# An attention-then-Fourier-mix kernel on one core: second weights loaded in two pairs, and the opening batches' steps put in another order

## The chip, the core and the metric

The kernel runs on one core of a Trainium2 chip. The metric is device time in microseconds; the kernel before took 309.74 us, the median of 8 runs (307.34 to 312.01). A core has TensorE (PE, matrix multiplies into PSUM), VectorE (DVE), ScalarE (ACT), GpSimd (POOL) and SyncE (SP). Each engine takes its own instructions in the program's order and waits for the others by semaphores. Transfers between DRAM and the on-chip SBUF are issued by SP, ACT and POOL, and all run on the same 16 DMA engines.

## The reference

```python
# attention between x (8,8,512,64) and state (8,8,32,64), per batch and head
a     = softmax(x @ state.T / 8);   xread = a @ state
a2    = softmax(state @ x.T / 8);   sread = a2 @ x
x2    = concat(xread, sread)            # -> (8, 544, 512), heads side by side
# Fourier mix and a two-layer network
u     = x2 + real(fft(fft(x2, axis=1), axis=2))
un    = (u - mean) / sqrt(var + 1e-6)   # over the last axis
out   = u + relu(un @ w_ch1) @ w_ch2    # w_ch1 512 x 2048, w_ch2 2048 x 512
```

## The kernel before, in words

The work goes batch by batch, 0 to 7. For one batch b:

- **Load.** `load_x(b)` (L121) issues seven DMAs on SP into one of two `xs` buffers, in rows of 256 bytes. POOL casts it to bf16 into one of two `xin` buffers (`cast_x`, L148; for batch 2 `cast_columns`, L1117). For batches 2 and up, `turned[b]` (L560) issues DMA transposes on SP that give `sT` (state) and `xT` (x).
- **Attention** (`attend`, L360). The first stream holds `scores(0)`, `scores(1)` (matmuls L437, exponential on ACT L442), then `turn_scores(1)`, `turn_scores(0)` (matmuls with the identity L449, copied by ACT L450). `turn_scores` needs both exponentials. The second stream holds the reads: `read_low` (xread L462 into PSUM tile `xrp`, divided by DVE L470/L471 into `XR`, then POOL copies 32 rows of it into `XT`, L519), `fold_low` on POOL (L523 to L531), two reads into `XF`, `sread_by_head` (its L489 on DVE overwrites the rows of `XR` that `XT` was copied from, so it waits for POOL), and a last read followed by `fold()` (L536), twelve DVE operations that use the symmetry of the Fourier sums, from L534 to L549. In batches 0 and 1 a `state_rows` step on ACT (L515) overwrites those rows of `XR`, and the fold needs it.
- **Fourier mix** (`transform`, L698). `over_s(0..3)` (matmuls L783 on the fold's parts, ACT copies L784), `over_d(0..1)` (L679/L680 into `yp`), DVE adds x into `U` (L684, L691), statistics (L337/L339), centring into `ub` (ACT L840 for batch 1, DVE L842 later), and `turn_u`, the transposition into `unT` (TensorE L851 and a copy L852 for batches 0 and 1, SP DMA L847 later). Per batch there are four 128-row tiles (k, r).
- **Layer 1** (`layer1`, L914). 16 steps. Batch 0 uses `quarter_step` (L931): step L[4r+i] takes 16 matmuls of 128x128 (L936) of tile r, then ACT's ReLU L938. Other batches take 4 matmuls of 128x512 (L926) and L928. Each needs a PSUM tile `ph`.
- **Layer 2** (`layer2`, L947). For tile i four steps q of four 128x512 matmuls (L990) add up in one PSUM tile `po`; the last calls `store` (L952), whose DVE operation L957 scales, adds `U` and frees `po`. The output goes by SP, direct (L961) or through `r_dram` (L971, L972). For batch 0 the steps are called M[4i+q].

`ph` and `po` share the pool `psF`, which has three buffers; `xrp`, `xfp` and batch 2's scores share `psX`, which has one; the rest share `psQ`, which has three.

**What sets the order.** Every engine's order is the order in which the Python code emits the calls. Up to the first layer-2 steps it is written out by hand, L1024 to L1222. From there on each pass b of the loop at L1224 calls `weave` (L998): each stream is a list of steps with a start and an end between 0 and 1; the steps are spread evenly in that interval, and all are emitted in order of their place. Pass b runs layer 2 of batch b-1, layer 1 of b, reads and transform of b+1, scores of b+2, and the load of b+3. In pass 1 the remaining layer-2 steps are M[7] to M[15] (`l2_now`, nine).

**Weights.** POOL issues them as DMAs that cast float32 to bf16: `first_weights` (L310) four loads of w1, `second_weights` (L323, DMA L325) four of w2, each reading 1 MB and writing 512 KB. A `tensor_copy` into the tile `gate` on POOL holds POOL's queue back until the tile named in it is there: L1131 for the last w1 load, L1166 for batch 2's x, L1171 for the last w2 load. M with q = 0 needs the first w2 load, q = 1 the second, and so on.

**State.** `turn_in_dram(lo, hi)` (L154) copies state rows in reversed order from DRAM to DRAM (`s_dram`), `load_state` (L112) brings them in (tile `gen`), POOL casts them into `stb` (L168). For batch 2 this happens early (SP at 12.0 and 20.7 us); for batches 3 to 7 the copy goes out at 28.3, the load at 32.6, and POOL casts it after L1171. The eight `root` calls (L343/L344 on POOL) that L957 of batches 0 and 1 need follow that.

Of the kernel before, what the change touches and what calls it, by code (L numbers as in the profile page):

```python
# [30 lines left out]
def kernel(  # L31
# [8 lines left out]
    nc = tc.nc  # L40
# [71 lines left out]
    def load_state(lo, hi, src=state):  # L112
        nc.sync.dma_start(
            out=states(lo, hi).rearrange("p b g d -> p (b g) d"),
            in_=src[lo:hi].rearrange("b (g hh) j d -> (hh j) (b g) d", hh=4),
        )
# [4 lines left out]
    def load_x(b):  # L121
        xs = xs_of[b] if b in xs_of else wk.tile([128, 4 * dm], F32, name="xs", tag="xs")
        xs_of[b] = xs
        v = xs.rearrange("p (i h d) -> p i h d", i=4, d=D)
        xb = x[b].rearrange("h s d -> s h d")
        row = v[15:32:16, 3]
        parts = [
            (v[:, 0], xb[1:129]),
            (v[:, 1], xb[144:272]),
            (v[:, 2], xb[273:401]),  # L130
            (v[32:128, 3], xb[416:512]),
            (v[0:15, 3], xb[129:144]),
            (v[16:31, 3], xb[401:416]),
            (row, xb[0:273:272]),
        ]
        if b == 0:
            for queue, n in ((nc.sync, None), (nc.scalar, 2), (nc.sync, 3), (nc.scalar, 0), (nc.sync, 4), (nc.sync, 5), (nc.sync, 6),
                             (nc.sync, 1)):
                if n is None:
                    load_state(0, 1)  # L140
                else:
                    queue.dma_start(out=parts[n][0], in_=parts[n][1])
            return
        for o, rows in parts:
            nc.sync.dma_start(out=o, in_=rows)  # L145

    def cast_x(b, copy=nc.gpsimd.tensor_copy, lo=0, hi=4):
        copy(xin_bufs[b % 2][:, lo:hi, 1:513], xs_of[b].rearrange("p (i c) -> p i c", i=4)[:, lo:hi])  # L148
# [5 lines left out]
    def turn_in_dram(lo, hi):  # L154
        nc.sync.dma_start(out=s_dram[lo:hi].rearrange("b h j d -> (b h) j d"),
                          in_=state[lo:hi, :, ::-1, :].rearrange("b h j d -> (b h) j d"))
# [151 lines left out]
    def first_weights(lo, hi):  # L308
        for q in range(lo, hi):
            nc.gpsimd.dma_start(out=w1[:, :, q * 512:(q + 1) * 512], in_=w1v[:, :, q * 512:(q + 1) * 512])  # L310
# [9 lines left out]
    for lo, k0, c, t in ((0, 0, 3, 128.0), (128, 128, 3, 128.0), (256, 0, 4, 256.0), (384, 128, 5, pf[:, 6:7])):  # L320
        nc.gpsimd.tensor_scalar(gi[:, lo:lo + 128], in0=li[:, k0:k0 + 128], scalar1=pf[:, c:c + 1], scalar2=t,
                                op0=ALU.mult, op1=ALU.add)
    def second_weights():  # L323
        for q in range(4):
            nc.gpsimd.dma_start(out=w2[:, q * 4:(q + 1) * 4, :], in_=w2v[:, q * 4:(q + 1) * 4, :])  # L325
    def clear_state(lo, hi):
        nc.gpsimd.memset(stb[:, lo:hi].rearrange("p b g c -> p (b g c)").bitcast(F32), 0.0)
# [30 lines left out]
    turned = {}  # L358
# [588 lines left out]
    def layer2(key):  # L947
        steps = []
        n = 1 if isinstance(key, tuple) else 4
        po_of = {}  # L950

        def store(i, cols):  # L952
            u, rstd, dst = tiles_of[key][i]
            while later:
                later.pop()()
            ot = wk.tile([128, dm], F32, name="ot", tag="ot", bufs=4)
            nc.vector.scalar_tensor_tensor(ot[:, cols], in0=po_of[i][:, 0:cols.stop - cols.start], scalar=rstd,  # L957
                                           in1=u[:, cols], op0=ALU.mult, op1=ALU.add)
            queue = nc.scalar if key == B - 1 else nc.sync
            if isinstance(dst, bass.AP):  # L960
                nc.sync.dma_start(out=dst[:, cols], in_=ot[:, cols])  # L961
            elif isinstance(dst, int):
                nc.sync.dma_start(out=l_dram[dst].rearrange("b r n -> (b r) n"), in_=ot)
                for a in range(2):
                    nc.sync.dma_start(out=out[4 * dst:4 * dst + 4, 129 + 272 * a:144 + 272 * a, :].rearrange("b r n -> r b n"),
                                      in_=l_dram[dst, :, 16 * a:16 * a + 15, :].rearrange("b r n -> r b n"))
                    nc.sync.dma_start(out=out[4 * dst:4 * dst + 4, 272 * a, :].rearrange("b (c n) -> c b n", c=16),
                                      in_=l_dram[dst, :, 16 * a + 15, :].rearrange("b (c n) -> c b n", c=16))
            else:
                b, k, top = dst  # L970
                queue.dma_start(out=r_dram[b, k], in_=ot)  # L971
                later.append(lambda: queue.dma_start(  # L972
                    out=out[b, top:top - 128:-1, :].rearrange("r (c n) -> c r n", c=16),
                    in_=r_dram[b, k].rearrange("r (c n) -> c r n", c=16)))

        def step(i, q):
            if key == B - 1 and i == n - 1:
                cols = slice(0, 384) if q < 2 else slice(384, 512)
                if q % 2 == 0:
                    po_of[i] = psF.tile([128, dm], F32, name="po", tag="c")  # L980
                for f in range(8 * (q % 2), 8 * (q % 2) + 8):
                    nc.tensor.matmul(po_of[i][:, 0:cols.stop - cols.start], lhsT=h_of[key][:, f, i * 128:(i + 1) * 128], rhs=w2[:, f, cols],  # L982
                                     start=(f == 0), stop=(f == FC - 1))
                if q % 2:
                    store(i, cols)
                return
            if q == 0:
                po_of[i] = psF.tile([128, dm], F32, name="po", tag="c")
            for f in range(4 * q, 4 * q + 4):
                nc.tensor.matmul(po_of[i], lhsT=h_of[key][:, f, i * 128:(i + 1) * 128], rhs=w2[:, f, :],  # L990
                                 start=(f == 0), stop=(f == FC - 1))
            if q == 3:
                store(i, slice(0, dm))

        return [lambda i=i, q=q: step(i, q) for i in range(n) for q in range(4)]
# [11 lines left out]
    def warm(n):  # L1007
        t = psF.tile([128, 512], F32, name="warm", tag="c")
        for i in range(n):
            nc.tensor.matmul(t[:, 0:128], lhsT=ident, rhs=ident, start=(i == 0), stop=(i == n - 1))  # L1010
# [56 lines left out]
    nc.gpsimd.tensor_add(ZB[0:32, 1, 0:1], XRs[0][0:32, 0, 128:129], XRs[0][0:32, 0, 384:385])  # L1067
    nc.gpsimd.memset(XB[0:32, 1, 257:258], 0.0)
    first_weights(3, 4)
    warm(4)  # L1070
    read(1)
    sread()
# [40 lines left out]
    L, M = layer1(0), layer2(0)  # L1113
    over_s1, over_d1, add1, centre1, turn_u1, done1 = transform(1)
# [15 lines left out]
    clear_state(3, B)  # L1130
    nc.gpsimd.tensor_tensor(gate, xs_of[0][:, 0:4], w1[:, :, 3 * 512], op=ALU.add)  # L1131
    load_x(2)
    turn_in_dram(3, B)
    turned[2, 0]()
    turn_u(0, 1)
    add_sums(0, 0)
    centre_sums(0, 0)
# [26 lines left out]
    r1[6]()  # L1164
    r1[7]()
    nc.gpsimd.tensor_copy(gate, xs_of[2].rearrange("p (i c) -> p i c", i=4)[:, :, 0])  # L1166
    second_weights()
    nc.gpsimd.tensor_copy(gate, XQs[1].rearrange("p (g j c) -> p g j c", g=2, j=4)[:, 1, 3, 0:4])
    for i in range(4):
        cast_columns(0, 508, slice(i, i + 1))  # L1170
# [19 lines left out]
    M[0]()  # L1190
    over_d1(0)
    add1(0, 1)
    centre1(0, 1)
    add1(0, 0)
    centre1(0, 0)
    L[12]()
    over_d1(1)
    add1(1, 1)
    L[13]()
    M[4]()  # L1200
    turn_u1(0, 1, nc.scalar.copy)
    L[14]()
    centre1(1, 1)
    add1(1, 0)
    centre1(1, 0)
    L[15]()
    turn_u1(0, 0, nc.scalar.copy)
    M[1]()
    turn_u1(1, 1)
    M[5]()  # L1210
    turn_u1(1, 0)
    spread(0, 0)
    spread(1, 1)
# [2 lines left out]
    state_blocks(3, B, nc.gpsimd.tensor_copy)  # L1216
    for root in first_roots[0:1] + first_roots[5:8] + first_roots[1:5]:
        root()
    M[2]()
    M[6]()  # L1220
    M[3]()
    done1()  # L1222
    l2, scores_first = M, scores_next
    for b in range(1, B + 1):  # L1224
        reads_next = reads_after
        l2, l2_now = (layer2(b), [l2[7]] + l2[8:]) if b == 1 else (layer2(b) if b < B else [], l2)
        streams = [(l2_now + (layer2(("L", b // 4)) if b in (3, 7) else []), 0, 1)]
        if b < B:
            streams.append((layer1(b), 0.13 if b == 2 else 0.08, 1))
        if b + 1 < B:  # L1230
            if b == 1:
                streams.append((scores_first[0:2], 0.03, 0.12))
                streams.append((scores_first[2:4], 0.12, 0.2))
            streams.append((reads_next, 0.2 if b == 1 else 0, 0.45 if b == 1 else 0.3))
            streams.append((transform(b + 1), 0.62 if b == 1 else 0.47, 0.9 if b == 1 else 0.85))
        if b + 2 < B:
            scores_next, reads_after = attend(b + 2)
            streams.append(([lambda: (cast_x(b + 2), turned[b + 2]())], 0.25, 0.25))
            streams.append((scores_next, 0.5, 1))
        if b + 3 < B:  # L1240
            streams.append(([lambda: load_x(b + 3)], 0.35, 0.35))
        if b in (3, 7):
            streams.append((low_rows(b // 4), 0.02, 0.2))
            streams.append((layer1(("L", b // 4)), 0.36, 0.8))
        weave(*streams)
# [30 lines left out]
```

## Time and profile before

| | |
|---|---|
| median of 8 runs | 309.74 us (307.34 to 312.01) |
| profiled execution: device time / span of its profile | 310.11 / 308.3 us |
| TensorE busy in the span | 292.7 us (95%) |
| DVE, ACT, POOL busy | 179.0, 135.5, 89.7 us |
| four matmuls of 128x512 (one step) back to back | 0.86 us |
| one w load, issue to landing | 6.8 to 12.2 us |
| w1 issued / w2 issued / last w2 landed | 10.0 to 14.5 / 32.7 to 35.7 / 47.2 us |
| first layer-2 matmul (M[0]) / end of M[3] | 39.52 / 56.07 us |

The profile is of one execution. A line of a timeline gives start, duration, engine, source line, operation, output and input, count, and in brackets how long the engine had been idle before it and what ended the idle time. A line of the waits view gives who waited for whom, the microseconds in total, how often, and the longest. A line of the windows view gives the busy time of PE, weight load, DVE, ACT and POOL in that stretch, then the TensorE clock that was granted (1.00 is full speed), the DMA engines' busy share and GB/s. In the slices each digit is the busy share of one fortieth of the span, in tenths. In the DMA queue lines, q0 holds POOL's transfers and q1 SP's: packets, megabytes, share of 16 engines.

### The profile page before, as it was taken

Reading aid. Unit: us, or ns where it says so; the run is one execution under the profiler, and the core shown is the slowest. Engines: PE = TensorE matmul, PEld = TensorE weight load, DVE = VectorE, ACT = ScalarE, POOL = GpSimd, SP = SyncE. Lnnn points to the kernel's source line nnn. Section 1 sums busy time; section 2 is a strip of 40 time slices with the busy share of each in tenths; the row PEclk is TensorE's granted clock in tenths of the full one; section 3 lists DMA queues with packets and bytes.
Section 4 is the critical chain, followed back from the end, with each engine's and each line's share of the span. In section 5 each row is a group of like instructions: output and inputs, shape, how many; then the busy total and the mean of one; then the engine's idle time right before and its main releaser. Section 6 shows DMA issues by size and latency. Waiting matters only on the chain.

```text
span 308.3 us, 6055 instructions
## 1 busy us (share of the span) xinstructions
PE 292.7 (95%) x2333; PEld 166.8 (54%) x2333; DVE 179.0 (58%) x446; ACT 135.5 (44%) x253; POOL 89.7 (29%) x222
## 2 busy tenths in 40 slices
PE   5999969996989999999999999999999999999996
PEld 5789946443544555456654454445444544555443
DVE  8868982467387575782917846684759383100112
ACT  6887745433543545235452455235533533333300
POOL 6766635660145022700307012700340041000000
PEclk9999997999899999999999999999999999999999
DMA  8998893868134794356652496444243023500345
GB/s 153 200 206 176 162 200 73 170 122 167 39 69 119 83 209 119 59 115 140 147 92 75 108 179 110 94 102 87 69 105 68 36 62 91 104 34 34 70 126 146
DMA packets 110794, 34.86 MB, mean 113 GB/s; under 512 B 101950, under 2 KB 106302, under 8 KB 110766
## 3 DMA queue, kind: packets, MB, share of 16 engines
q1 hardware_dynamic: 100046, 28.72, 43.7%
q0 software_dynamic: 4224, 4.19, 8.4%
q10 hardware_dynamic: 6496, 1.57, 2.5%
q8 instruction: 18, 0.29, 0.4%
q14 instruction: 10, 0.08, 0.1%
HBM read 22.41 MB, written 14.02 MB: 118 GB/s over the span
## 4 chain that ended last, share of the span: by engine, by line
PE 77%; DMA 8%; DVE 7%; POOL 2%; SPq 2%; ACT 1%; issue 1%; ACTq 0%; POOLq 0%; DVEq 0%
PE po L990 35%; PE ph L926 31%; DMA s_dram<-in_state_dram 3%; PE gp L783 2%; DMA w<-in_moe_w_ch_dram 2%; DMA xs<-in_x_dram 2%; DMA gen<-s_dram 2%; SPq L145 2%; DVE st L337 1%; DVE U L684 1%; PE po L982 1%; PE yp L680 1%; PE yp L679 1%; PE esp L437 1%; PE ph L936 1%; PE xrp L462 1%
## 5 line engine op out<-in xcount | busy, mean ns | idle before, releaser
L990 PE MATMUL po<-w,hT 128*128 128x512 bf16 x496 | 124.7, 381 | 2.8 <-ACT hT L938 2.5
L928 ACT ACTIVATE hT<-ph 128x512 bf16<-128x512 f32 x112 | 66.9, 597 | 125.9 <-PE ph L926 125.9
L926 PE MATMUL ph<-unT,w 128*128 128x512 bf16 x448 | 115.2, 381 | 2.5 <-DVE ot L957 2.5
L926 PEld LDWEIGHTS <-w 128*128 128x128 bf16 x576 | 50.8, 98 | 49.8 <-issue 3.9
L990 PEld LDWEIGHTS <-hT 128*128 128x128 bf16 x496 | 46.8, 98 | 50.2 <-issue 3.4
L957 DVE SCALAR_TENSOR_TENSOR ot<-po,rstd,U 128x512 f32<-128x512 f32 (+2 forms) x33 | 24.1, 731 | 51.0 <-PE po L990 48.9
L787 POOL COPY GL<-G 128x128 bf16<-128x128 bf16 x7 | 2.0, 289 | 78.0 <-ACT G L784 78.0
L684 DVE TENSOR_TENSOR U<-yp,XR 128x512 f32<-128x512 f32 x14 | 9.5, 682 | 25.8 <-PE yp L680 25.8
L337 DVE BATCH_NORM_STATS2 st<-U 128x6 f32<-128x512 f32 x32 | 21.8, 682 | 0.1
L344 POOL TENSOR_TENSOR rstd<-rstd,mhalf 128x1 f32<-128x1 f32 x34 | 20.1, 590 | 2.7
L343 POOL TENSOR_TENSOR rstd<-mv,epst 128x1 f32<-128x1 f32 x34 | 6.6, 194 | 45.1 <-DVE mv L339 44.9
L936 PE MATMUL ph<-unT,w 128*128 128x128 bf16 x256 | 17.2, 225 | 1.0 <-ACT hT L938 0.7
L936 PEld LDWEIGHTS <-w 128*128 128x128 bf16 x256 | 15.9, 101 | 1.4 <-issue 1.2
L784 ACT CAST G<-gp 128x288 bf16<-128x288 f32 x28 | 13.0, 482 | 4.2 <-PE gp L783 4.1
L842 DVE TENSOR_SCALAR ub<-U,mv 128x512 bf16<-128x512 f32 x24 | 12.3, 513 | 0.9
L938 ACT ACTIVATE hT<-ph 128x512 bf16<-128x512 f32 x16 | 9.4, 593 | 5.5 <-PE ph L936 5.5
L148 POOL CAST xin<-xs 128x2048 bf16<-128x2048 f32 (+1 forms) x9 | 11.7, 1317 | 0.0
L519 POOL COPY XT<-XR 32x514 bf16<-32x514 bf16 x7 | 4.2, 602 | 24.9 <-DVE XR L471 24.9
L442 ACT ACTIVATE E<-esp 128x512 bf16<-128x512 f32 x14 | 8.4, 597 | 4.9 <-PE esp L437 4.9
L471 DVE TENSOR_TENSOR XR<-xrp,rs 128x512 bf16<-128x512 f32 x14 | 9.7, 695 | 0.5
L471 DVE TENSOR_TENSOR XF<-xfp,rs 128x512 bf16<-128x512 f32 x14 | 9.7, 692 | 0.5
L462 PEld LDWEIGHTS <-ET 128*128 128x128 bf16 x56 | 4.9, 98 | 8.4 <-DVE XR L471 2.1
(245 smaller groups left out, 376.8 us busy)
## 6 DMA issues: line engine op xcount, KB each, us to landing
xs<-in_x_dram SPq DMA_DIRECT2D x22, 256.0 KB, 4.3
w<-in_moe_w_ch_dram POOLq DMA_DIRECT2D x8, 512.0 KB, 9.6
out_dram<-ot SPq DMA_DIRECT2D x15, 256.0 KB, 3.8
r_dram<-ot SPq DMA_DIRECT2D x14, 256.0 KB, 2.2
out_dram<-r_dram SPq DMA_DIRECT2D x14, 256.0 KB, 3.6
xs<-in_x_dram SPq DMA_DIRECT2D x8, 192.0 KB, 4.6
xs<-in_x_dram ACTq DMA_DIRECT2D x2, 256.0 KB
l_dram<-ot SPq DMA_DIRECT2D x2, 256.0 KB, 2.0
```

The source lines that it names most:

```text
L148: copy(xin_bufs[b % 2][:, lo:hi, 1:513], xs_of[b].rearrange("p (i c) -> p i c", i=4)[:, lo:hi])
L337: nc.vector.bn_stats(st6, u)
L344: nc.gpsimd.tensor_tensor(rstd, rstd, mhalf, op=ALU.pow)
L471: nc.vector.tensor_tensor(ov, in0=p[ps, :, 0:256].rearrange("p g (h d) -> p g h d", d=D), in1=rs[ps].unsqueeze(3).to_broadcast([n, 2, 4, D ...
L684: nc.vector.tensor_add(u.rearrange("p (k r) -> p k r", r=2), p.rearrange("p (r k) -> p k r", r=2)[:, 0:u.shape[1] // 2, :], x.rearrange("p ...
L784: nc.scalar.copy(G[:, j, :].rearrange("p (i q) -> p q i", q=2), p[:, 0:NM].rearrange("p (q i) -> p q i", q=2))
L842: nc.vector.tensor_scalar(t, in0=ud, scalar1=mv[:, 0:1], scalar2=None, op0=ALU.subtract)
L926: nc.tensor.matmul(ph[:, o:o + n], lhsT=w1[:, c, f * 128:(f + 1) * 128], rhs=un_of[key][:, c, :], start=(c == 0), stop=(c == DC - 1))
L928: nc.scalar.activation(hT[:, per * i:per * i + per, :].rearrange("p a b -> p (a b)"), ph, AF.Relu, scale=-1.0 / 512 if key == 0 else -1.0 ...
L936: nc.tensor.matmul(ph[:, o:o + 128], lhsT=w1[:, c, f * 128:(f + 1) * 128], rhs=un_of[key][:, c, 128 * r:128 * r + 128], start=(c == 0), st ...
L957: nc.vector.scalar_tensor_tensor(ot[:, cols], in0=po_of[i][:, 0:cols.stop - cols.start], scalar=rstd, in1=u[:, cols], op0=ALU.mult, op1=AL ...
L990: nc.tensor.matmul(po_of[i], lhsT=h_of[key][:, f, i * 128:(i + 1) * 128], rhs=w2[:, f, :], start=(f == 0), stop=(f == FC - 1))
```

## The change

Four things are edited; no instruction's work changes, only places do.

1. `second_weights` takes a range. Two of its loads are issued directly after the last w1 load, ahead of POOL's gate L1094; the other two stay behind the gate on batch 2's x.
2. Batch 2's state transposes (`turned[2, 0]`) go ahead of the DRAM copy of the later batches' state on SP.
3. In the part written by hand, L[12] and L[13] are emitted ahead of batch 1's centrings of tiles (0, 1) and (0, 0), M[1] ahead of `turn_u1(0, 0)`, L[15] ahead of the last centring, and M[2] ahead of the last `turn_u1`.
4. In the loop, pass 1's layer-2 steps are split: five of them, M[7] to M[11], in 0 to 0.38, four, M[12] to M[15], in 0.6 to 1. Scores, reads and transform of batch 2 get slightly earlier places, and the next x's cast and transposes move from 0.25 to 0.15 in pass 1 and to 0.2 in later passes.

Seen engine by engine, the program after has these differences: on POOL the cast of batch 3's x comes ahead of XT's copy (L519) of batch 2; on ACT the ReLU of L[12] comes ahead of both centrings, that of L[13] between them; on DVE the closing operation of batch 0's tile 2 comes ahead of batch 2's last read and fold; on SP batch 0's third output goes ahead of batch 4's x load.

```diff
-    def second_weights():
-        for q in range(4):
+    def second_weights(lo, hi):
+        for q in range(lo, hi):
             nc.gpsimd.dma_start(out=w2[:, q * 4:(q + 1) * 4, :], in_=w2v[:, q * 4:(q + 1) * 4, :])
...
     first_weights(3, 4)
+    second_weights(0, 2)
...
     load_x(2)
+    turned[2, 0]()
     turn_in_dram(3, B)
-    turned[2, 0]()
...
-    second_weights()
+    second_weights(2, 4)
...
     add1(0, 1)
+    L[12]()
     centre1(0, 1)
+    over_d1(1)
     add1(0, 0)
+    L[13]()
     centre1(0, 0)
-    L[12]()
-    over_d1(1)
     add1(1, 1)
-    L[13]()
     M[4]()
     turn_u1(0, 1, nc.scalar.copy)
     L[14]()
     centre1(1, 1)
     add1(1, 0)
+    M[1]()
+    turn_u1(0, 0, nc.scalar.copy)
+    L[15]()
     centre1(1, 0)
-    L[15]()
-    turn_u1(0, 0, nc.scalar.copy)
-    M[1]()
+    M[5]()
     turn_u1(1, 1)
-    M[5]()
+    M[2]()
     turn_u1(1, 0)
...
-    M[2]()
     M[6]()
     M[3]()
...
+        if b == 1:
+            streams = [(l2_now[:5], 0, 0.38), (l2_now[5:], 0.6, 1)]
...
-                streams.append((scores_first[0:2], 0.03, 0.12))
-                streams.append((scores_first[2:4], 0.12, 0.2))
-            streams.append((reads_next, 0.2 if b == 1 else 0, 0.45 if b == 1 else 0.3))
-            streams.append((transform(b + 1), 0.62 if b == 1 else 0.47, 0.9 if b == 1 else 0.85))
+                streams.append((scores_first[0:2], 0, 0.08))
+                streams.append((scores_first[2:4], 0.08, 0.15))
+            streams.append((reads_next, 0.17 if b == 1 else 0, 0.42 if b == 1 else 0.3))
+            streams.append((transform(b + 1), 0.58 if b == 1 else 0.47, 0.88 if b == 1 else 0.85))
...
-            streams.append(([lambda: (cast_x(b + 2), turned[b + 2]())], 0.25, 0.25))
+            streams.append(([lambda: (cast_x(b + 2), turned[b + 2]())], 0.15 if b == 1 else 0.2, 0.2))
```

## The prediction

> **What bounds the kernel now.** I read the page's slices first, then TensorE's waits, then the timelines of ACT, DVE, POOL and the DMA queues around the waits. The slices show a TensorE that is full from slice 13 on (about 92 us), and two dips of PE and PEclk before that, slices 6 and 10:
>
> ```profile
> PE   5999969996989999999999999999999999999996
> ...
> PEclk9999997999899999999999999999999999999999
> ```
>
> So time is won or lost only in what TensorE does before 92 us. Its waits:
>
> ```profile
> PE ph L926 <- DVE ot L957: 2.5, 1, 2.5
> PE po L990 <- ACT hT L938: 2.5, 1, 2.5
> PE xfp L462 <- DVE XR L471: 1.0, 1, 1.0
> PE ph L936 <- ACT hT L938: 0.7, 1, 0.7
> PE xrp L462 <- ACT ET L450: 0.7, 1, 0.7
> PE po L990 <- DMA w<-in_moe_w_ch_dram: 0.3, 1, 0.3
> ```
>
> Each long wait is a PSUM buffer of psF (three in all) that an engine gives back late. Layer-2 step M[4] (43.2 to 45.7) needs the buffer of L[12], whose ReLU stands on ACT behind two centrings that wait for DVE's statistics:
>
> ```profile
> 42.69 0.72 ACT L840 ACTIVATE ub<-U,mv 128x512 bf16<-128x512 f32 x1 [2.97 <-DVE mv L339]
> 44.46 0.72 ACT L840 ACTIVATE ub<-U,mv 128x512 bf16<-128x512 f32 x1 [1.05 <-DVE mv L339]
> 45.09 1.06 ACT L938 ACTIVATE hT<-ph 128x512 bf16<-128x512 f32 x2
> ```
>
> The other (72.8 to 75.4) is a layer-2 result whose closing operation (L957) queued on DVE behind the whole fold of batch 2, 69.3 to 74.6:
>
> ```profile
> 69.30 0.70 DVE L534 TENSOR_TENSOR Sm<-XF,XR 128x1028 bf16<-128x1028 bf16 x1
> ...
> 72.17 0.43 DVE L543 TENSOR_TENSOR XQ<-XE 128x256 bf16<-128x256 f32 x1
> ...
> 74.58 0.75 DVE L957 SCALAR_TENSOR_TENSOR ot<-po,rstd,U 128x512 f32<-128x512 f32 x1
> ```
>
> After each, TensorE ran at half clock for a stretch (PEclk, the ninth figure, 0.51): 3.4 us at half speed lose 1.7 us more.
>
> ```profile
> 45.90:49.30 3.40, 3.40 (x24) 2.54 (x23) 1.60 (x4) 0.84 (x2) 2.00 (x6) 0.51 0.31 59
> ...
> 76.60:80.00 3.40, 3.40 (x26) 2.30 (x24) 0.00 (x0) 2.15 (x6) 0.00 (x0) 0.51 0.42 107
> ```
>
> **What the skill says.** The Trainium skill, "TensorE: Matmul & The Clock Gate", section "What's actually happening", gives a free-running window of about 3.4 us, an idle one halving the clock and a busy one restoring it. The trace agrees in length, but 2.2 to 2.6 us idle in a window was enough here, and 1.0 us (90.5 to 91.5) was not. "PSUM — Partial Sum Buffer", "Engine vs sequencer instructions": ScalarE, VectorE and GpSimdE queues are strict FIFO; the ACT lines above are that. "DMA: Bandwidth & Descriptors", "Queues, rings and completion order": each DMA engine alternates between queues packet by packet. The trace is harsher to SP's queue (q1, small packets): between 22 and 23 us, beside the first weights on q0, it got 13 packets, and after q0 ran dry 3464 in 4 us (24.5 to 28.5).
>
> ```profile
> q0 software_dynamic: 202, 0.20, 122.3%
> ...
> q1 hardware_dynamic: 13, 0.00, 1.6%
> ```
>
> **Part 1: two w2 loads right after the last w1 load.** POOL issues two more DMAs at 14.5, 2 x 0.76 (3.02 for four at 32.7) = 1.5 us, hidden in its 2.5 us wait ahead of L1094 (17.0); uncovered it would delay batch 1's casts by 1.5. A w load is 528 packets, at 202 per us 2.6 us; q0 now runs dry at about 29.5 instead of 24.3. Until then SP's queue starves. Batch 2's state load (issued 20.7) landed at 25.6, just as q0 thinned. Its bounds are 25.6 and 30.8 (+5.2); a copy of the same 64 KB made beside w1 took 8.7 us, which would give 29.4. I take 30.0, +4.4. POOL waits for it:
>
> ```profile
> 25.74 1.27 POOL L168 CAST stb<-gen 32x128 bf16<-32x128 f32 x4 [3.85 <-DMA gen<-s_dram]
> ...
> 28.89 0.60 POOL L519 COPY XT<-XR 32x514 bf16<-32x514 bf16 x1
> ...
> 32.57 0.18 POOL L1166 COPY gate<-xs 128x4 f32<-128x4 f32 x1
> ```
>
> XT's copy then ends at 33.9, not 29.5. ACT's L515 (31.75), which overwrites the rows XT copies, must wait: +2.2, behind it ReLUs that TensorE's buffers absorb (about 0.3 lost). The fold of batch 1 (L534, 32.95) needs L515: +1.65. TensorE's over_s(0) at 36.40 follows that fold without a gap, so with the slack between over_s and M[0] (about 0.3) the path loses 1.4 and wins 0.3 since M[0] finds w2 landed: M[0] at 40.6 instead of 39.5. Bounds of the loss: 0 (state by 27.8) to 2.5.
>
> Batch 2's x lands near 35; POOL reaches its gate only at 37 anyway. The second pair is issued at 37, moves from 39.5 (32.7 to 35.2 was the like delay) to 44.7 and lands at 45.5 (the last w2 landed at 47.2 before).
>
> **Part 2: state transposes ahead of the state's DRAM copy on SP.** Batch 2's x leaves SP at about 33.3; two transposes take 3.3; so the copy (1280 packets, about 2.5 us alone, landed 32.6) goes out at 36.6 into the second pair's traffic: landing about 45.7. The load behind it and then batch 2's x transposes follow: these start at 46.3, before 47.58 (where they waited for the last w2). First two land 3.7 later (1.27 apart, 2.4 each) = 50.0, all by 52.6. Batch 3's x lands 12 after their start (59.5 before, by the last packets) = 58.3; the rest of the state lands near 50.3, POOL casts it (3.0) and runs the eight roots (0.78 each) to 59.5.
>
> **Part 3: L ahead of the centrings.** ReLU L[12] now precedes both centrings: M[4] finds its buffer, and TensorE never reaches the half-clock stretch. Left: L[14] and L[15] wait for ReLUs behind a centring and a copy, 0.1 and 0.3. Gone: 2.5 + 0.7 + 1.7. M[3] ends near 52.6 instead of 56.07 (40.6 + 11.6 of work, which is 56.07 - 39.52 less the 4.9, + 0.4). The x transposes, needed by scores(1) at 53.7 and in by 52.6, still hide.
>
> **Part 4: the weave.** (a) Turn_scores(1) now follows scores(1) with no layer-1 step between. Before, matmuls to transposed use took 0.86 (57.40 to 58.26) under one step; now open: +0.9, and the wait of 0.7 at xrp is covered by a step instead. (b) Tile 2 of batch 0 closes before the fold, tile 3 after: the 2.5 and the 1.7 behind L926 go. (c) But between batch 2's last read and over_s(0) stand now three layer-1 steps and a score, 3 x 0.86 + 0.23 = 2.8; before it was four and two layer-2 steps, 5.4. From the last read's reciprocal to XQ's first part took 4.3 us (68.33 to 72.60), from the matmul another 0.4: TensorE waits 4.7 - 2.8 = 1.9, and 0.4 at over_s(2): +2.3 near 68. Bounds 1.5 to 4. Whether this idles a clock window decides another 1.7; I count half, 0.85. (d) POOL's cast of batch 3's x now stands ahead of XT's copy, and DVE's L489 waits for XT. By the numbers above the cast ends at 61.4, XT at 62.0, and L489 could start at 62.3: nothing, with 0.3 to spare. (e) The 1.0 at xfp: eight steps instead of seven between over_d and the read (0.86 more cover): 0.3 left.
>
> The earlier casts of later batches (0.2 for 0.25) also move out_dram issues behind transposes on SP; their x landed a stage before, and TensorE has no wait after 92 us: 0, at worst a few tenths.
>
> **Sum** against the profiled execution (310.11, span 308.3, so 1.8 around it): removed 0.3 + 4.9 + 0.7 + 4.2 + 1.0 = 11.1; added 1.4 + 0.4 + 0.9 + 2.3 + 0.85 + 0.3 = 6.15; net 5.0: 305.1. The median is 0.37 lower: 304.7, span near 303.3.
>
> **Rivals.** *Clean*: the state lands early, the clock holds, or the fold's gap is smaller: up to 2.4 + 0.85 back: 301.4 to 303. For it: 1.0 idle at 91 us left the clock alone; against: the small copy's 8.7 us under w1. *DMA order eats it*: SP's copy crawls beside q0 (between 16 and 20 us q1 moved 264 packets: 19 us for 1280, though q0 lasts only 5.2), the x transposes start at 49 to 52, and each us past 47.4 stands open at scores(1): 306.5 to 309.5. For it: those 264; against: most of the copy can pass before the second pair starts (39.5). *Buffers still bind*: the PSUM wait moves to L[14] or L[15] with half its size and the clock drop: about 308. For it: still three buffers; against: the ReLUs' places on ACT. *Slower*: POOL's FIFO at (d). If batch 3's x lands late, cast, XT, L489, second xfp and the fold move one for one, TensorE idling through it at half clock after. It costs from x's landing at 60, and the gain is gone at 65 (64 if the clock drop is certain); 67 would give 312. For it: the wait is in the program, and x hangs on part 2's order; against: x would have to land 7 us later than worked out.
>
> **Numbers.** Likeliest as summed, 302.7 to 306.7: 0.50; clean 0.15; DMA order 0.17; buffers 0.08; slower than before 0.10, of which most lies past 1%. About 1% is what a measurement of this kernel can tell from no change. Faster by over 1% (under 306.6): 0.64; within: 0.28; slower: 0.08. Leaving out the fast half of clean and the slow tail gives 301.5 to 309.5.
>
> **What would show it.** Right: no wait L990 <- ACT hT and none L926 <- DVE ot; PEclk 1.0 through 42 to 52; a wait gp L783 <- DVE XQ of about 2; eTp <- ACT E near 0.9; POOL's stb wait up from 3.85 to near 8; SP's x transposes start at 46 or so. Wrong: over_s(0) of batch 1 no later than 36.4 (part 1 too dear), transposes past 48, L489 waiting for POOL over 1 us, or waits after 92 us.

## The result and the profile after

The changed kernel takes 305.47 us (median of 21 runs, 303.24 to 309.21) against 308.55 us for the kernel before on the same chips (56 runs): ratio 0.989, 95% interval 0.987 to 0.992, so about 1.1% or 3.3 us faster (3.1 between the medians). 304.7 was forecast. Of the 21 executions nine had a mean granted clock of about 1.00 and took 304.2 us on average, six had 0.994 and took 305.8, and six had 0.989 and took 308.3; the profiled one (308.16 us, 2.7 above the median) is of the last six. It is read here for places and waits; what it loses to the clock is not lost in every execution.

The slices, counted from 1. The clock dips in slice 8 only, where it dipped in 7 and 11 before (the prediction's "slices 6 and 10" are those of the PE row):

```profile
PE   5999998798999999999999999999999999999996
...
PEclk9999999699999999999999999999999999999999
```

TensorE's waits of more than a tenth in the changed stages:

```profile
PE esp L437 <- DMA xT<-xin: 2.9, 3, 1.4
PE gp L783 <- DVE XQ L543: 1.9, 2, 1.3
PE eTp L449 <- ACT E L442: 0.5, 1, 0.5
...
PE xfp L462 <- DVE XR L471: 0.2, 1, 0.2
```

Neither of the two waits of 2.5 us is left, nor the one for weights. In their place stands one that was not there before: the scores of batch 2 (L437) wait 2.9 us for its x transposes. The chain of waits says why (start, duration, what):

```profile
38.93 9.81 DMA s_dram<-in_state_dram
...
48.76 0.41 SPq L113
...
49.35 1.23 SPq L388
...
53.23 2.50 DMA xT<-xin
...
55.78 0.62 PE esp L437 x8
```

SP's queue runs in order. The state load (L113) waits for the DRAM copy to land, which took 9.81 us, and the x transposes (L388) stand behind that load: they start at 49.35, where 46.3 was forecast and 47.58 was before. TensorE, waiting twice 1.4 us, then falls to half clock (the granted clock is the third number from the end: 0.72, 0.50, 0.78):

```profile
53.80:57.20 3.40, 1.50 (x15) 0.75 (x14) 1.52 (x5) 0.93 (x2) 3.06 (x7) 0.72 0.57 126
57.20:60.60 3.40, 3.40 (x11) 1.27 (x11) 0.71 (x2) 1.28 (x3) 3.06 (x9) 0.50 1.30 220
60.60:64.00 3.40, 3.40 (x19) 1.78 (x18) 0.90 (x2) 1.28 (x3) 3.04 (x5) 0.78 0.33 95
```

So the forecast time came out of a different bill than the one forecast. What is new on the bill in this profile: 2.9 us of waits on x; 3.4 x 0.50 + 3.4 x 0.22 = 2.4 us of clock in the last two stretches (the first, at 0.72, is left out because PE was busy for only 1.5 of its 3.4 us); 1.9 us at the folds of batches 1 and 2; 0.5 at the scores' transposes.

### The profile page after: what moved, and what is told of

Same layout as the page of the kernel before. It is cut to its first block, busy times and chain, and to the rows that moved or that the text cites. A ratio compares the mean times of both kernels' runs of the same rounds, so it can differ in the third digit from the quotient of the medians.

```text
span 306.4 us, 6054 instructions
## 1 busy us (share of the span) xinstructions
PE 292.8 (96%) x2333; PEld 165.0 (54%) x2333; DVE 179.4 (59%) x446; ACT 136.4 (45%) x253; POOL 92.6 (30%) x222
## 3 DMA queue, kind: packets, MB, share of 16 engines
q0 software_dynamic: 4224, 4.19, 8.4%
## 4 chain that ended last, share of the span: by engine, by line
PE 75%; DMA 11%; DVE 5%; SPq 4%; POOL 3%; issue 1%; ACT 0%; ACTq 0%; POOLq 0%
PE po L990 34%; PE ph L926 32%; DMA s_dram<-in_state_dram 6%; PE gp L783 2%; DMA gen<-s_dram 2%; DMA xs<-in_x_dram 2%; SPq L145 2%; SPq L388 1%; PE po L982 1%; PE xfp L462 1%; PE yp L680 1%; PE esp L437 1%; PE eTp L449 1%; PE yp L679 1%; DVE U L684 1%; DMA xT<-xin 1%
## 5 line engine op out<-in xcount | busy, mean ns | idle before, releaser
L926 PEld LDWEIGHTS <-w 128*128 128x128 bf16 x576 | 50.9, 98 | 47.9 <-issue 2.0
L936 PE MATMUL ph<-unT,w 128*128 128x128 bf16 x256 | 16.4, 219 | 0.3 <-DVE unT L852 0.3
L936 PEld LDWEIGHTS <-w 128*128 128x128 bf16 x256 | 15.1, 98 | 0.6 <-issue 0.4
L519 POOL COPY XT<-XR 32x514 bf16<-32x514 bf16 x7 | 4.2, 604 | 22.8 <-DVE XR L471 22.8
L471 DVE TENSOR_TENSOR XR<-xrp,rs 128x512 bf16<-128x512 f32 x14 | 9.7, 694 | 0.5
L471 DVE TENSOR_TENSOR XF<-xfp,rs 128x512 bf16<-128x512 f32 x14 | 9.7, 692 | 0.5
L684 DVE TENSOR_TENSOR U<-yp,XF 128x510 f32<-128x510 f32 x14 | 9.4, 673 | 0.0
```

The costliest lines, as they stand in the source:

```text
L471: nc.vector.tensor_tensor(ov, in0=p[ps, :, 0:256].rearrange("p g (h d) -> p g h d", d=D), in1=rs[ps].unsqueeze(3).to_broadcast([n, 2, 4, D ...
L684: nc.vector.tensor_add(u.rearrange("p (k r) -> p k r", r=2), p.rearrange("p (r k) -> p k r", r=2)[:, 0:u.shape[1] // 2, :], x.rearrange("p ...
L926: nc.tensor.matmul(ph[:, o:o + n], lhsT=w1[:, c, f * 128:(f + 1) * 128], rhs=un_of[key][:, c, :], start=(c == 0), stop=(c == DC - 1))
L936: nc.tensor.matmul(ph[:, o:o + 128], lhsT=w1[:, c, f * 128:(f + 1) * 128], rhs=un_of[key][:, c, 128 * r:128 * r + 128], start=(c == 0), st ...
```

## Experiments

Each of the twelve was timed beside the kernel before, whose median there was 307.67 to 309.18 us; so the ratio is the safer number when kernels of different experiments are compared. T1 was my first theory: the changed kernel could be faster still, and what costs it is the late start of the x transposes, caused by both load edits (the split of the second weights, called Part 1 in the prediction, and the later copy, Part 2). T2 was its rival: these edits are worth their place, and undoing them loses. Later theories are numbered on, and each expectation says what its theory holds.

**The copy back ahead of the state transposes** (Part 2 undone)

```diff
     load_x(2)
-    turned[2, 0]()
     turn_in_dram(3, B)
+    turned[2, 0]()
```

> The changed kernel with one part taken back: the state's DRAM copy is issued ahead of batch 2's state transposes again, the second weights stay split in two pairs. T1 (the end of the x transposes sets the loss: they start at 49.35 us in the changed kernel, because the copy is issued at 38.93 and lands beside the second weights' last pair at 48.76): the copy is now issued ahead of the two state transposes (which took 2.58 us), so at about 36.5, and lands about 2 us earlier; the x transposes start at 47.0 to 47.5 (then held by the gate on the last weights, 47.4), the two waits on xT before scores(0) and scores(1) of batch 2 fall from 2.9 to about 1.4 us in all, the half clock from 57 to 60.6 us goes, and the time is 1.5 to 3 us below the changed kernel's (302.5 to 304). T2 (the waits on xT are only taken from a wait that would stand elsewhere): the transposes move but the time stays within 1 us of the changed kernel's, 305.5.

Measured 303.49 us, ratio 0.984 (0.980 to 0.988), against 0.989 (0.987 to 0.992) for the changed kernel: 2.0 us by the medians, with intervals that just overlap; the next pair of kernels shows the same edit more clearly. SP's timeline of this kernel (start, duration, line):

```profile
34.32 0.81 SPq L155 DMA_DIRECT2D s_dram<-in_state_dram  x1
35.23 3.42 SPq L377 DMA_TRANSPOSE sT<-stb  x2
38.76 0.62 SPq L113 DMA_DIRECT2D gen<-s_dram  x1
46.28 5.13 SPq L388 DMA_TRANSPOSE xT<-xin  x4
```

The copy now takes 38.76 - 34.32 = 4.4 us in place of 9.8: it runs in a hole. Between 34 and 39 us the DMA engines' busy share was 0.55 here and 0.34 in the changed kernel, where the copy stood behind two transposes until the last pair of weights was issued. (Of the 4.6 us by which it goes out earlier, 2.6 are these transposes; the rest is x2's issue, which ended later in the changed kernel's profiled execution.) Batch 2's scores wait 0.28 us for x instead of 2.92 (about 1.4 was expected), and the clock is 1.00 from 55 to 65 us (0.66 in the changed kernel). The two profiled executions lie 6.0 us apart (302.11 and 308.16), the medians 2.0, so the usual sizes are smaller than these two profiles show; but five of this kernel's six executions had a clock of about 1.00, against nine of 21. T1 holds for Part 2.

**All four weight loads back behind the gate** (Part 1 undone, the later copy kept)

```diff
-    second_weights(0, 2)
...
-    second_weights(2, 4)
+    second_weights(0, 4)
```

> The changed kernel with the other part taken back: all four loads of the second weights stand behind the gate on batch 2's x, as before; the copy stays behind the state transposes. T1 (putting a pair ahead of x2 starves SP's queues, x2's issue takes 13.99 us in place of 6.91 and everything behind it on SP is late): SP's x2 issue takes about 7 us again, the copy goes out at about 31 and lands by 36, batch 1's fold no longer meets the POOL copies of 33 to 37 us (the wait of 0.54 us before the fold's column sums goes), the x transposes start at 47.2 to 47.6, M[0] waits about 0.3 us for the weights, and the time is 1.5 to 3 us below the changed kernel's (302.5 to 304). T2 (the early pair is what lets M[0], M[4] and M[1] run ahead): PE waits for the second weights by over 1 us at M[0] at 40 us, and the time is 0.5 to 2 us above the changed kernel's.

Measured 308.01 us, ratio 1.000 (0.996 to 1.003). T1 is wrong here: the copy did go out early (31.38 us) and batch 1's fold was not late, yet the x transposes started at 50.61, later than ever. What held them is the gate on the last weights, on POOL, and M[0] waited as well:

```profile
50.25 0.19 POOL L1171 CAST gate<-w 128x4 f32<-128x4 bf16 x1 [9.39 <-DMA w<-in_moe_w_ch_dram]
```
```profile
40.52 1.02 PE L990 MATMUL po<-w,hT 128*128 128x512 bf16 x4 [1.37 <-DMA w<-in_moe_w_ch_dram]
```

The copy and the load behind it ran beside four weight loads, and the last of these landed 2.3 us later than in the next kernel, which has the copy 3.2 us earlier. T2's number (0.5 to 2 us above the changed kernel) was passed: 2.5.

**Only the two orders** (Parts 1 and 2 both undone; diff: both of the above)

> The changed kernel with both loads and copy taken back: only the order of batch 1's steps and of the first loop round is the changed kernel's. T1: the gain is all in the orders, and the loads' parts cost about 1.7 us: the time is 1.5 to 3 us below the changed kernel's (302.5 to 304; ratio to the kernel before 0.980 to 0.985), with the copy issued at 28.3, the fold of batch 1 not late and the x transposes at 47.2 to 47.6. T2 (the parts are meant to be together): M[0] or the scores wait for loads by over 2 us and the time is at or above the changed kernel's 305.5.

Measured 304.82 us, ratio 0.989 (0.983 to 0.994), the same as the whole change. So no gain of the two load edits together can be seen. Against the kernel above, which differs only in where the copy stands, it is 3.2 us faster, with intervals that do not overlap: that is Part 2's cost where the weights stay together. The last gate opens at 47.98 us, the transposes start at 48.34, the scores of batch 2 wait 1.8 us, and M[0] waits 0.89 us for weights. The longer of the two waits on x:

```profile
54.76 0.51 PE L437 MATMUL esp<-sT,xT 128*128 128x64 bf16 x8 [1.48 <-DMA xT<-xin]
```

T1's 302.5 to 304 was too low: it had not seen that the gate alone already holds PE. T2's wait of over 2 us for loads did come (2.7 in all), and its 305.5 lies within the interval. Whether the split helps once the copy goes early stays open: with it (the first experiment) the last gate opens 2.1 us sooner, at 45.91, and the time is 1.3 us lower, but the intervals overlap.

**Only the order of batch 1's steps** (Part 3 alone, put into the kernel before)

> The kernel before with only the hand-written order of batch 1's steps from the changed kernel (layer 1 steps ahead of the centrings, M[1] and M[2] ahead). T1: the wait of PE for hT at the end of the hand-written stage (2.5 us and 0.7 us) and the half clock behind it (1.7 us) go; the wait for DVE's ot (2.5 us) and its half clock (1.7 us) in the loop's first round stay. Time 303.7 to 305.5 (ratio 0.984 to 0.990). T2 (the wait for hT only moves to the scores or to the second weights, since the steps run earlier than the loads allow): M[0] to M[2] or scores(0) wait by over 2 us more and the time is within 1 us of before, 308.5.

Measured 306.01 us, ratio 0.992 (0.989 to 0.995), half a microsecond above T1's range. All waits for hT and the half clock at 45.9 to 49.3 are gone (3.2 and 1.7 us), but 2.0 us come back at once as waits for batch 2's x, because PE now reaches the scores before the transposes that start at 47.51:

```profile
51.28 0.29 PE L437 MATMUL esp<-sT,xT 128*128 128x64 bf16 x4 [0.53 <-DMA xT<-xin]
53.90 0.41 PE L437 MATMUL esp<-sT,xT 128*128 128x64 bf16 x8 [1.47 <-DMA xT<-xin]
```

T1 had also expected the wait for ot and its half clock to stay; the wait shrank to 1.56 us and no half clock followed it. This gave T3: each edit frees PE, and then the start of the x transposes binds.

**Only the first loop round** (Part 4 alone, put into the kernel before)

> The kernel before with only the first loop round's edits (batch 0's last layer 2 steps in two groups, scores, reads and fold of batch 2 earlier). T3 (new: the steps and the loop round each shrink their own waits, but the steps alone ran PE ahead into 2.8 us of waits on batch 2's x transposes): here PE is not ahead, so the waits on xT stay near nothing, the wait for hT (2.5 us) and its half clock (1.7 us) stay, the wait for ot (2.5 us), its half clock (1.7 us), xrp (0.7 us) and most of xfp (1.0 us) go, and something of up to 1.5 us appears at the fold: time 303.5 to 305.5 (ratio 0.985 to 0.990). T4 (the two parts aren't independent: what the round saves is small): 307 to 308.5, ratio 0.995 to 1.0.

Measured 305.94 us, ratio 0.992 (0.989 to 0.995): between T3's 0.985 to 0.990 and T4's 0.995 to 1.0, with the wide part of the interval in neither. The waits for ot and xrp are gone, hT's stay, the fold waits 0.8 us. Steps alone gain 2.5 us and the round alone 2.6; together they gain 3.5, not 5.1, though the intervals are wide enough (1.9 to 5.2) that this shortfall alone proves nothing; the wait of batch 2's scores for x in the profiles does (none before, 2.0 us with the steps alone, none with the round alone, 1.8 with both).

**Only the split of the second weights** (Part 1 alone, put into the kernel before)

> The kernel before with only the second weights' split: two loads ahead of batch 2's x, two behind its gate. T3 (the split spreads the weights' bytes into a stretch of idle DMA, so the last pair lands about 2 us earlier, 45.5 to 46 in place of 47.2, but here PE comes late to the scores anyway, behind its 2.5 us wait for hT): M[0]'s wait of 0.3 us goes, the x transposes start about 1.5 us earlier at 46, the time is 307.5 to 308.6 (ratio 0.997 to 1.0). T1 as first put (the split starves SP and costs): x2's issue takes 13 to 14 us in place of 6.91, batch 1's fold is late by 0.5 to 2 us, and the time is 309.5 to 311.

Measured 308.18 us, ratio 0.999 (0.996 to 1.002): nothing, as T3 said (M[0]'s wait for weights is gone; the x transposes started at 47.03, not near 46). SP's x2 issue took 13.13 us, so the starving is real, but nothing on PE's path depends on it here; PE comes late to the scores anyway, behind its wait of 2.5 us for hT.

**The copy further ahead, in front of batch 2's x**

```diff
-    load_x(2)
     turn_in_dram(3, B)
+    load_x(2)
     turned[2, 0]()
```

> The changed kernel with the state's copy moved the other way still: ahead of batch 2's x load on SP, not only ahead of the state transposes. T3 (the bytes ahead of the last weights set when the x transposes start; the copy's bytes in front of x2 only delay x2, the gate and the last pair): the copy is issued at about 21.3, x2 lands 1 to 2 us later than with the copy behind it, the last gate on the weights ends at 47 to 47.5 in place of 45.9, and the time is 0.5 to 2 us above that of the copy behind x2 (304 to 305.5). T2 (what matters is only that the copy is out of the way of the last pair): the last gate comes at 44.5 to 45.5 and the time is at or below 303.5.

Measured 308.11 us, ratio 0.998 (0.996 to 1.001): 4.6 us slower than with the copy behind x2, over twice what T3 had allowed. The direction and the chain are T3's: x2 lands late (POOL waits 4.08 us at its gate, to 39.26), so the last pair is issued late and the last gate comes at 49.16, 3.2 us later; the transposes start at 49.53, the scores wait 3.1 us and the clock falls to 0.66 for 10 us. The sizes failed: the gate came 2 us later than I had worked out, and I had priced the delay without the clock behind it.

```profile
39.26 0.19 POOL L1167 COPY gate<-xs 128x4 f32<-128x4 f32 x1 [4.08 <-DMA xs<-in_x_dram]
...
49.16 0.19 POOL L1172 CAST gate<-w 128x4 f32<-128x4 bf16 x1 [5.71 <-DMA w<-in_moe_w_ch_dram]
```

**Copy ahead of the state transposes, and no hold on the x transposes**

The kernel casts 508 of the 512 columns of batch 2's x early and the last four only behind POOL's gate on the last weights. The transposes need all columns, so this gate holds them back; it is called the hold below.

```diff
-        cast_columns(0, 508, slice(i, i + 1))
-    nc.gpsimd.tensor_copy(gate, w2[:, 12:16, 0])
-    cast_columns(508, 512, slice(0, 4))
+        cast_columns(0, 512, slice(i, i + 1))
```

> The changed kernel with the copy ahead of the state transposes and without the hold on batch 2's x transposes: their cast is made in whole columns, so they no longer start behind the last weights. T3 (the hold is needed: 16 DMA engines are full between 39 and 47 us, so what starts earlier there only delays the weights): the transposes start at 41.5 to 42.5, run slower, the last weights land at 48 to 51 and M[2] or M[3] waits 1 to 3 us for them; time 304 to 306. T5 (the scores are bound by the transposes' start, and they fit beside the weights): scores(0) and scores(1) don't wait and the time is 302 to 303.3.

Measured 301.93 us, ratio 0.979 (0.975 to 0.982), and the narrowest spread of all (301.82 to 302.30). T5 is right, T3's fear wrong: the transposes start at 40.14 beside the weights and hold SP for 10.8 us, twice the usual 5.1, but the scores of batch 2, at about 51 us, don't wait for them, and no layer-2 step waits for weights: from 40 us on there is time for both. This is 6.3 us below the kernel before. Beside the first experiment, which differs in the hold alone, it is 1.6 us, with intervals that overlap.

```profile
39.04 0.53 SPq L113 DMA_DIRECT2D gen<-s_dram  x1
40.14 10.80 SPq L388 DMA_TRANSPOSE xT<-xin  x4
```

**The changed kernel with the state load behind the x transposes**

```diff
-    load_state(3, B, s_dram)
     turned[2]()
+    load_state(3, B, s_dram)
     load_x(3)
```

> The changed kernel with one order on SP's queue turned: batch 2's four x transposes are issued ahead of the load of the rest of the state, which waits for the copy. T3 (in the changed kernel it is this load, at 48.76 us, that holds the x transposes in SP's queue past the last weights' gate, which opened at 47.43): the transposes start at 47.8 to 48.0, the load goes out behind them at 53, the waits on xT before scores(0) and scores(1) fall from 2.9 to 1.5 to 2.2 us, and the time is 0.7 to 2 us below the changed kernel's (303.5 to 304.8). T1b (the bytes in flight, not the queue's order, hold them): the transposes run slower or start as late, and the time stays within 0.5 us of 305.5.

Measured 310.84 us, ratio 1.007 (1.004 to 1.009): slower than before, neither theory's number. The place was T3's (transposes at 48.14, waits on x 2.0 us), but I had forgotten who waits for the load. POOL casts the state as soon as it lands, and behind this cast stand in POOL's order the eight roots that batch 0's closing operations need:

```profile
57.12 2.98 POOL L168 CAST stb<-gen 32x640 bf16<-32x640 f32 x4 [8.78 <-DMA gen<-s_dram]
```
```profile
62.13 1.87 PE L990 MATMUL po<-w,hT 128*128 128x512 bf16 x4 [4.39 <-DVE ot L957]
```

A 320 KB load that nobody on PE wants for a long time cost 4.4 us of PE through one in-order queue, and half clock after it (0.55 and 0.50 from 55 to 65 us). The Trainium skill, "PSUM — Partial Sum Buffer", section "Engine vs sequencer instructions", calls the GpSimdE queue strict FIFO; this is that. In the changed kernel this cast starts at 52.28 and the roots run from 55.36; DVE waits 4.0 us for them there, PE not yet.

**The changed kernel without the hold** (copy kept late; diff of the hold as above)

> The changed kernel, its copy behind the state transposes kept, without the hold on the x transposes (batch 2's cast in whole columns). T3 (with the copy late, SP's wait for it at the state's load is what binds, and the hold is open by then): the transposes still start at 48.8 to 49.4 and the time stays within 0.7 us of the changed kernel's, 304.8 to 306.2. T5 (the hold alone costs): they start at 42 to 44 and the time falls to 302 to 303.3, as with the copy ahead.

Measured 305.09 us, ratio 0.988 (0.984 to 0.993), the changed kernel's time. With the copy late the hold is not what binds: the transposes stay behind the state load (49.60) and start at 50.17. T3 is right, and this separates the two locks on the same door: to come to 301.93, late copy and hold must both go.

**The kernel before without the hold**

> The kernel before without the hold on batch 2's x transposes and with nothing else changed. T3 (before, PE comes to scores(0) late, held by its wait for hT, so an earlier x is of no use): the transposes start at 40.5 to 43, M[0] waits 1 to 3 us for the second weights that now share the DMA engines with them, and the time is 308.3 to 310.5 (ratio 1.0 to 1.007). T5 (the hold costs wherever it stands): 305 to 307.3.

Measured 308.64 us, ratio 0.999 (0.996 to 1.001). T3 again: the transposes started at 39.22, but PE comes late, held by hT, and M[0] waits 1.05 us for weights. The same edit is worth nothing here and nothing with the late copy, 1.6 us beside the copy-first kernel, and 2.9 us beside the two orders (next).

**Only the two orders, without the hold** (loads as before)

> Only the two orders of the change (batch 1's steps and the first loop round), the loads as before, and without the hold on batch 2's x transposes: the fastest version so far (301.93) with the second weights' split taken out. T6 (the split is what makes room: without it four weight loads and the x transposes share the DMA engines from 39 us on, and M[0] to M[3] wait for weights): PE waits for the second weights for 1 to 3 us in all, the weights land at 49 to 51, and the time is 303.3 to 305.5 (ratio 0.983 to 0.990). T7 (the split is of no use once the hold is gone): 301.5 to 302.7, no more than 0.5 us of waits for weights.

Measured 301.93 us, ratio 0.980 (0.976 to 0.985). T7: with the hold gone no use of the split can be seen; PE waits 0.48 us for weights at M[0], and that is all. T6's 1 to 3 us did not come. The transposes start early, and no score of batch 2 waits for them:

```profile
39.53 6.30 SPq L388 DMA_TRANSPOSE xT<-xin  x4
```

Against the two orders with the hold (304.82) this is 2.9 us by the medians and about 2.5 by the ratios, whose intervals just overlap. Executions of like clock separate it better: at about 1.00 the two orders took 303.7 to 304.3 us with the hold (three executions) and, in five of six, 301.3 to 302.0 without it. The difference fits the 1.8 us of waits; the rest of the 2.9 would then be half clock, which none of these six had. The hold also kept POOL's queue: its cast of the later state moves from 48.48 to 41.34 us. PE waits for nothing behind that cast in either kernel. What is left is a wait of 0.97 us for batch 3's x transposes, at 67.15.

The kernels with both orders, by the start of batch 2's x transposes in their profiled execution, with that execution's own time:

| kernel | transposes start | PE waits for batch 2's xT | clock, 55 to 65 us | this execution | median |
|---|---|---|---|---|---|
| orders, no hold | 39.53 | 0 | 1.00 | 301.9 | 301.93 |
| copy first, no hold | 40.14 | 0 | 1.00 | 302.0 | 301.93 |
| copy first | 46.28 | 0.28 | 1.00 | 302.1 | 303.49 |
| orders only | 48.34 | 1.82 | 0.83 | 305.4 | 304.82 |
| the change | 49.35 | 2.92 | 0.66 | 308.2 | 305.47 |
| copy ahead of x2 | 49.53 | 3.12 | 0.66 | 308.1 | 308.11 |
| the change, no hold | 50.17 | 4.19 | 0.66 | 308.7 | 305.09 |
| weights together | 50.61 | 3.45 | 0.83 | 307.8 | 308.01 |

In these executions a start up to about 46.3 us is nearly free, and 3 us of lateness from there go with 6 us of time: the clock (and in three kernels 1.3 to 1.5 us at the fold of batch 2) adds as much as the waits. By the medians the loss is smaller and less regular, 1.3 to 4.6 us above copy first, since the executions profiled of the change, with and without the hold, are 2.7 and 3.6 us above their medians.

The executions of one kernel differ by up to 6 us, and in large part this is the clock. A stretch of 3.4 us at half clock costs 1.7 us, or 0.006 of the span, so the changed kernel's mean clocks of 1.00, 0.994 and 0.989 fit none, one and two such stretches, and their mean times lie 1.6 and 2.5 us apart. The twelve executions of the first two kernels of the table all stayed at about 1.00, between 301.28 and 303.78 us. Why one execution of a kernel meets half clock and another does not, these runs do not show: of each kernel only one execution was profiled. It would fit that the DMA traffic falls a little differently in each and moves the transposes' start; that stays a guess.

## Why the prediction was right, and where it was not

**The time** (304.7 forecast, 305.47 measured, within the likeliest case's own 302.7 to 306.7) was right, the direction too. The places of the losses were half wrong, and that the total is near is in part luck.

**What it removes, 11.1 us: right.** The waits for hT, ot, xrp and w2 are gone, xfp fell from 1.0 to 0.2, and PEclk is 1.00 between 45.9 and 49.3. The single-part kernels show that the two orders do it. Only the 0.3 for weights is the split's: M[0] waits 0.89 us with the orders alone and not at all with the split alone.

**Part 1, "the path loses 1.4": too dear.** The small state load landed with POOL's cast at 27.87 (30.0 forecast; 25.74 before), and XT's copy at 31.12 left ACT's L515 alone. PE waits 0.54 us at batch 1's fold, M[0] is at 39.78 (40.6 forecast, 39.52 before). And even this 0.54 came by another way than the one I gave, through POOL and DVE slowing each other, as shown at the end. The second pair was issued at 38.34 (37 forecast), its gate ended at 47.43 (45.5 forecast, 47.22 before): the split's own gain was eaten.

**Part 2, "landing about 45.7 ... these start at 46.3": the step that failed.** The mechanism I had named as the rival "DMA order eats it" is what happened, at the lower end of its place (49 to 52); its time (306.5 to 309.5) holds for the profiled execution, not for the median. The copy's 9.8 us in flight are close to the 9.1 I had given it; but it went out at 38.93 and not at 36.6 (37.2 and 37.4 in the two other kernels with this head), since x2's issue held SP for 13.99 us (6.91 before), and it ran its full length beside the last weights: in the changed kernel without the hold it took 12.2 us, from 37.43 to 49.60. I had given nothing to "each us past 47.4 stands open at scores(1)" in the sum, as I had them start at 46.3. Measured in the profile: 2.9 us of waits and 2.4 of clock. In the nine executions with a mean clock of about 1.00 hardly any of the second part can have been lost.

**Part 3: right, and better.** M[3] ends near 51.25 (its last two steps start at 49.53 and take 0.86 each; 52.6 forecast, 56.07 before); the 0.4 at L[14] and L[15] did not come. Just this brought PE to the scores early and so made Part 2 matter.

**Part 4:** (a) 0.9 forecast, 0.5 measured. (b) right. (c) 2.3 forecast near 68 us; 1.32 came, at 74.38, with no clock drop, so the half-counted 0.85 was not due there. (d) no wait: POOL's cast ended at 63.85 and XT's copy at 64.5, both 2.5 us later than worked out, but DVE's L489 waited for its own matmuls until 67.01. The rival "Slower" had no part in this. (e) 0.16 for 0.3.

**The sum** had 6.15 us added: 1.4 + 0.4 + 0.9 + 2.3 + 0.85 + 0.3. The profile has 0.54 + 0 + 0.5 + 1.32 + 0 + 0.16 = 2.5 of these, and 5.3 at the x transposes that the sum did not have: 7.8 in all. Two errors offset each other: the six terms were 3.6 us too dear together, and one of 5.3 was missing. The sum was made for the profiled execution, and there it missed: 305.1 forecast, 308.16 measured. The span fell by 1.9 us, where 11.1 - 7.8 gives 3.3. Of the 1.4 left, at most 0.28 x 3.4 = 0.95 can lie in the stretch at clock 0.72 that is not counted above; the rest I can't assign. The median came near because most executions lose less clock than the profiled one, before and after. The 3.4 us of half clock that the sum takes away are also those of one execution: of 30 executions of the kernel before that were timed beside the first experiments, ten had a clock of about 1.00 already (307.5 us on average), eleven 0.994 (308.6) and nine 0.989 (310.2).

## What to carry to other kernels

When an edit lets the busiest engine run ahead, ask at once what it will now arrive at too early; here a hold that was free before became the bound. Taking it out was worth 2.9 us beside the two orders (301.93 against 304.82), which themselves gave 3.5, and nothing in the kernel before or beside the late copy. A small transfer moved back in an in-order queue is priced not by its bytes but by what it then runs beside and by all that stands behind its consumer: the copy behind two transposes cost 2 to 3 us, and a postponed state load stopped PE for 4.4 us through POOL's roots. With the weights split it did best in a stretch where the DMA engines had room (a share of 0.34 between 34 and 39 us without the copy); further ahead, in front of batch 2's x, it cost 4.6 us.

## What the runs showed of the hardware

DVE's fold and POOL's four operations for XQl, which all read and write SBUF, slow each other when they run at the same time. In the kernel with only the two orders POOL's four operations for XQl end before DVE's fold begins. Two of each, POOL then DVE (start, duration):

```profile
31.90 0.45 POOL L530 TENSOR_TENSOR XQl<-XOl 32x128 bf16<-32x128 f32 x1
32.32 0.40 POOL L531 TENSOR_TENSOR XQl<-XOl 32x128 bf16<-32x128 f32 x1
```
```profile
34.29 0.69 DVE L540 TENSOR_TENSOR SS<-Sm 128x514 f32<-128x514 bf16 x1
35.01 0.69 DVE L541 TENSOR_TENSOR XE<-SS 128x512 f32<-128x512 f32 x1
```

In the changed kernel, POOL being 2 us late, they coincide, and both take longer:

```profile
34.87 0.90 POOL L530 TENSOR_TENSOR XQl<-XOl 32x128 bf16<-32x128 f32 x1
35.73 0.85 POOL L531 TENSOR_TENSOR XQl<-XOl 32x128 bf16<-32x128 f32 x1
```
```profile
34.52 0.94 DVE L540 TENSOR_TENSOR SS<-Sm 128x514 f32<-128x514 bf16 x1
35.49 0.83 DVE L541 TENSOR_TENSOR XE<-SS 128x512 f32<-128x512 f32 x1
```

All four POOL operations double (two are shown), the two of DVE grow by 0.14 and 0.25 us, and the fold's first result comes 0.7 us later after its start: that is batch 1's wait of 0.54 us, which I had forecast from a late L515 (it ran at 31.77, as before). With the copy first only the last two POOL operations meet the fold, and exactly these take 0.94 and 0.85. It is not every overlap: POOL's 0.45 at 31.90 ran beside DVE's L471, which reads PSUM, unharmed. The Trainium skill, "GPSIMD Engine Reference", section "Architecture", says that POOL's SBUF ports are shared with DVE; that section gives no price, and here it is about 0.45 us for each such POOL operation.

Half clock followed the waits on x in some kernels and not in others: with the steps alone PE idled 2.0 of the 8 us from 47 to 55 and kept 1.00, in the kernel of the two orders it idled 1.8 us and fell to an average of 0.83 over the next 10. The total idle in the stretch doesn't decide it; how the idle falls on the windows may, which these runs do not show.
